# Two element-wise operations moved from POOL to VectorE, row factors in three buffers, and the feed-forward stream at two steps a turn

## The chip, the cores and the metric

The kernel runs on one core of one Trainium2 chip. The metric is the device time of one execution in microseconds (us). The kernel before took 1141.61 us, the median of 3 runs (1139.79 to 1145.35). The engines are called as in the profile: PE is TensorE (PEld its weight loads), DVE is VectorE, ACT is ScalarE, POOL is GpSimd, and SP is the engine that issues most of the loads.

## The reference

The computation is an attention with a small memory, followed by a feed-forward layer for a part of the tokens. There are 8 batches, 8 heads, 576 positions, a head size of 64 and 32 memory slots; the second part works on rows of 512 numbers, with a hidden size of 1024 and a capacity of 128 tokens for each batch.

```python
a = softmax(phi, axis=positions)            # 8 x 8 x 576 x 32
k_m = einsum('bhsm,bhsd->bhmd', a, k)       # 32 x 64 for each head
v_m = einsum('bhsm,bhsd->bhmd', a, v)
x = softmax(q @ k_m.T / 8) @ v_m            # laid out as 8 x 576 x 512
scores = x @ w_gate
for b in range(8):
    top = the 128 tokens with the highest scores[b]
    xe = x[b, top]
    out[b] = x[b]
    out[b, top] = xe + sigmoid(scores[b, top]) * (relu(xe @ w1) @ w2)
```

Which tokens are chosen depends on small differences of the scores, so the kernel computes the first softmax and `v_m` in more than plain single precision, by splitting numbers into a high and a low part.

## The kernel before, in words

The work is a set of Python generators. One main loop advances each of them by a step or a few in every turn, and the order in which they issue instructions is the program order of every engine. That order is fixed when the kernel is built: a turn is a list of work for DVE, ACT, PE, POOL and SP, and each engine walks through its own list, waiting where it needs another's result.

**The streams of a turn.**

- `softmaxes` runs the softmax over positions for 16 groups (batch and half of the heads, a tile of 128 rows by 576 positions) and then `keys`. The first 8 groups are handled by two chains with scratch of their own (`ex0`, `ex1`), taking turns; the last 8 by the first chain alone. A group takes 11 steps. Its four extended-precision multiply-adds are `fma` (L214 to L223), which use the scratch tiles `lo`, `big` and `low`: five operations on DVE, and one product on POOL (L218). DVE reads that product in L222.
- `keys` (L298) transposes the softmax on PE, copies it to `aS` on ACT, splits it on DVE into `ahi` and `alo` (L312, L314), and writes both to `aparts` in DRAM by eight transfers issued on POOL (L317). PE forms `k_m` from `aS` (L323).
- `split_v` splits `v` of a group in a high part (L285, DVE) and the rest (L287, a subtraction on POOL), and writes both to `vparts` in DRAM (L290). It takes a step every second turn while both it and the softmaxes are under way.
- `values` (run by `all_sums`) sums `v_m` for a set of two batches as a chain of small matmuls (L360), one position after the other, 8 matmuls a step. Its operands are rows of factors that SP loads in pieces of `T` = 24 positions: one transfer for `v_rows` (L340) and four for `a_rows` (L347). There are two buffers of each, and the load of the next piece is issued when a piece begins. A turn takes 7 steps of it, or 9 when the softmaxes are done. There are four sets.
- `attentions` runs a batch through `centre`, `scores`, `attend`, `rank` and `gather`, 26 steps. Two batches can be under way; the second starts 12 turns after the first, or 8 when the softmaxes are done. `attend` has an addition on POOL (L522). `gather` fetches the 128 chosen rows by an indirect transfer and appends the batch to `chosen`.
- `ffns` takes a batch from `chosen`, passes three empty steps, and runs `ffn`: transposes (L605), 16 matmuls with `w1` (L616), transposes again, 16 matmuls with `w2` (L626), an update on DVE (L629) and an indirect transfer of the rows to the output. That is about 24 steps with the empty ones. A turn takes one step of it, or two when more than one batch is waiting. What is left when the attentions are done follows without anything between.

The part of the main loop that counts here:

```python
for _ in range(STEPS + 2 * (not working)):
    next(sums, None)
...
if attend_all and next(attend_all, working) is working:
    break
for _ in range(1 + (len(chosen) > 1)):
    next(products)
```

Of the kernel before, what the change touches and what calls it, by code (L numbers as in the profile page):

```python
# [9 lines left out]
F32 = mybir.dt.float32  # L10
F16 = mybir.dt.float16
F32R = mybir.dt.float32r
# [4 lines left out]
ALU = mybir.AluOpType  # L17
# [3 lines left out]
P = 128  # L21
NC = 6
# [16 lines left out]
def kernel(  # L39
# [14 lines left out]
    nc = tc.nc  # L54
    ctx.enter_context(tc.manual_schedule())
    B, S, D = out.shape
    PT = S // NC
# [5 lines left out]
    Dh = D // H  # L63
    M = P // 4
    F = w1.shape[1]
    KD, KF = D // P, F // P
    SET = 2
    T = 24
    scale = 1.0 / Dh ** 0.5
    out_flat = out.rearrange("b s d -> (b s) d")  # L70

# [7 lines left out]
    rows = ctx.enter_context(tc.tile_pool(name="rows", bufs=1))  # L79
# [40 lines left out]

    v_rows = [rows.tile([P, T, Dh], F32R, name=f"v_rows{i}") for i in range(2)]
    a_rows = [rows.tile([P, 4, T, M], F32R, name=f"a_rows{i}") for i in range(2)]
    for t in v_rows + a_rows:
        nc.gpsimd.memset(t.bitcast(F32), 0.0)
    for t in kbd + vbd + vls:
# [50 lines left out]

    tt, stt = nc.vector.tensor_tensor, nc.vector.scalar_tensor_tensor
    soft = {}  # L180

    def softmax(i, ch):

        ex = exs[ch]

        def t(name, dtype=F32):
            return ex.tile([P, S], dtype, name=name)

        r = phis.pop(i)
        mx = ex.tile([P, 1], F32, name="mx")  # L190
# [9 lines left out]
        rh, rl = t("rh", I16), t("rl")  # L200
# [13 lines left out]
        def fma(val, h, c):  # L214


            lo, big, low = t("lo"), t("big"), t("low")
            nc.gpsimd.tensor_tensor(out=low, in0=val, in1=rl, op=ALU.mult)  # L218
            stt(out=lo, in0=val, scalar=GRID, in1=h, op0=ALU.mult, op1=ALU.subtract)  # L219
            tt(out=lo, in0=lo, in1=rh, op=ALU.mult)  # L220
            tt(out=big, in0=h, in1=rh, op=ALU.mult)
            tt(out=low, in0=low, in1=lo, op=ALU.add)  # L222
            stt(out=val, in0=big, scalar=c * UP, in1=low, op0=ALU.add, op1=ALU.add)  # L223

# [17 lines left out]
        dl, p = t("lo"), t("big")  # L242
# [35 lines left out]
    def split_v(b):  # L278

        for g in range(NG):  # L280
            vb = vio.tile([P, 4 * S * Dh // P], F32, name="vb")
            nc.sync.dma_start(out=vb, in_=v[b, g])
            yield
            hi = vio.tile([P, 4 * S * Dh // P], F32, name="vhi")
            nc.vector.tensor_single_scalar(hi.bitcast(I32), vb.bitcast(I32), -4096,  # L285
                                           op=ALU.bitwise_and)
            nc.gpsimd.tensor_sub(vb, vb, hi)  # L287
            yield
            for vp, src in enumerate((vb, hi)):
                nc.gpsimd.dma_start(  # L290
                    out=vparts[b, g, :, vp].rearrange("w r s d -> w (r s d)")
                                           .rearrange("w (p x) -> p w x", p=P),
                    in_=src.unsqueeze(1).to_broadcast([P, 2, 4 * S * Dh // P]))
            yield
# [3 lines left out]
    def keys(i, ch):  # L298
        ex, (b, g) = exs[ch], groups[i]
        a = soft.pop(i)  # L300
        kb = ks.pop(i)
        aS = ex.tile([PT, NC, P], F32, name="aS")
        for c0 in range(0, NC, 3):
            tp = bank([PT, 3, P])
            for c in range(3):
                nc.tensor.transpose(out=tp[:, c], in_=a[:, (c0 + c) * PT:(c0 + c + 1) * PT],  # L306
                                    identity=ident)
            nc.scalar.activation(aS[:, c0:c0 + 3], tp, AF.Copy)  # L308
        yield
        hi = ex.tile([PT, NC, P], F32, name="ahi")  # L310
        lo = ex.tile([PT, NC, P], F32, name="alo")
        nc.vector.tensor_single_scalar(hi.bitcast(I32), aS.bitcast(I32), -4096,  # L312
                                       op=ALU.bitwise_and)
        nc.vector.tensor_sub(lo, aS, hi)  # L314
        for part, src in enumerate((lo, hi)):
            for h in range(4):
                nc.gpsimd.dma_start(  # L317
                    out=aparts[h, b, g, part].rearrange("(c p) m -> p c m", p=PT),
                    in_=src[:, :, h * M:(h + 1) * M])
        km = bank([P, 2, 2 * M])  # L320
        for rr in range(2):
            for c in range(NC):
                nc.tensor.matmul(out=km[:, rr], lhsT=kb[:, c, rr * P:(rr + 1) * P],  # L323
                                 rhs=aS[:, c, rr * 2 * M:(rr + 1) * 2 * M],
                                 start=(c == 0), stop=(c == NC - 1))
        for u in range(2):
            part = slice(u * Dh, (u + 1) * Dh)
            nc.scalar.activation(kbd[b][part, 2 * g:2 * g + 2, u * M:(u + 1) * M],
                                 km[part, :, u * M:(u + 1) * M], AF.Copy)
# [3 lines left out]
    def values(st):  # L333

        b0 = st * SET

        def load(ch):
            nc.sync.dma_start(  # L340
                out=v_rows[ch % 2][0::2].rearrange("p s d -> p (s d)").bitcast(F32),
                in_=vparts[b0:b0 + SET].rearrange("b g t w r s d -> (b g t w r) (s d)")
                    [:, ch * T * Dh:(ch + 1) * T * Dh])
            for h in range(4):
                src = aparts[h, b0:b0 + SET].rearrange("b g t s m -> (b g t) (s m)")
                src = src[:, ch * T * M:(ch + 1) * T * M]
                nc.sync.dma_start(  # L347
                    out=a_rows[ch % 2][2 * h::8, h].rearrange("p s m -> p (s m)").bitcast(F32),
                    in_=src.unsqueeze(1).to_broadcast([4 * SET, 2, T * M]))

        n = S // T
        load(0)
        for ch in range(n):
            if ch + 1 < n:
                load(ch + 1)
            vr, ar = v_rows[ch % 2], a_rows[ch % 2]
            for s in range(T):
                for i in range(2 * SET):
                    p = slice(i * 32, i * 32 + 32)
                    nc.tensor.matmul(out=accs[i][:Dh, :P].rearrange("p (h m) -> p h m", m=M),  # L360
                                     lhsT=vr[p, s], rhs=ar[p, :, s],
                                     start=(ch == 0 and s == 0), stop=(ch == n - 1 and s == T - 1))
                if s % 2:
                    yield
        for bb in range(SET):
            v_m[b0 + bb] = const.tile([P, NPR, M], F32, name=f"v_m{b0 + bb}")
            for g in range(NG):
                for u in range(2):
                    nc.scalar.activation(
                        v_m[b0 + bb][u * Dh:(u + 1) * Dh, 2 * g:2 * g + 2],  # L370
                        accs[2 * bb + g][:Dh, :P].rearrange("p (r u m) -> p r u m", r=2, u=2)[:, :, u],
                        AF.Copy)
# [278 lines left out]
    chosen, done = [], []  # L651
# [71 lines left out]
    while True:  # L723
# [23 lines left out]
            attend_all = attentions()  # L747
        if attend_all and next(attend_all, working) is working:
            break
        for _ in range(1 + (len(chosen) > 1)):  # L750
            next(products)
    done.append(True)
    finish(products)
# [47 lines left out]
```

## Time and profile before

| | |
|---|---|
| time, median of 3 runs | 1141.61 us (1139.79 to 1145.35) |
| span of the profiled execution | 1141.4 us |
| mean granted TensorE clock | 0.805 |
| moved by the DMA engines | 156.64 MB, 137 GB/s over the span |
| SP's loads of `v_rows` / `a_rows` | 96 of 384 KB / 384 of 48 KB |
| POOL's writes of `vparts` / `aparts` | 32 of 1152 KB / 128 of 72 KB |

The profile is a record of one execution. Its page gives the busy time of each engine, the span in 40 slices with the busy share of each engine in tenths, the chain of work that ended last, and the costliest groups of instructions. A group's line reads: source line, engine, operation, tile written and tile read, shapes and count; then the busy time in us and the mean of one instruction in ns; then the idle time of the engine just before these instructions, and what ended it. The trace behind the page can be asked for a table of stages (stretches of the span, with the busy time of each engine), for waits in a stretch, and for a timeline: one line for each instruction or run of like instructions, with its start in us, its duration, and in brackets the idle time before it.

The span falls into four stages. Up to about 430 us two softmax chains run. From 430 to 845 us one chain runs beside attentions. From 845 us the softmaxes are done, and the last set of `values` runs beside the attentions of batches 4 and 5, until 1018 us. Then come the attentions of batches 6 and 7, and two feed-forward blocks, which run from 1091 to 1128 us with nothing beside them.

### The profile page before, as it was taken

The numbers are of one execution on the slowest core, as the hardware profiler recorded it, in microseconds if no ns is written. First come the engines' busy times: TensorE is split into PE (matmuls) and PEld (weight loads), VectorE is DVE, ScalarE is ACT, GpSimd is POOL, SyncE is SP. The second block draws the span as 40 slices with busy tenths as digits, with TensorE's granted clock in tenths as the row PEclk, the third lists the DMA queues.
The fourth block names the chain that finished last, engine by engine and source line by source line (L and its number), as shares of the span: only waits on it lengthen the run. The fifth ranks groups of instructions, "written<-read, shape, count | busy, mean of one in ns | idle before, by whom it ended". The sixth has DMA issues, their size and how long they took to land.

```text
span 1141.4 us, 25115 instructions
## 1 busy us (share of the span) xinstructions
PE 605.3 (53%) x10738; PEld 428.4 (38%) x10738; DVE 789.0 (69%) x1227; ACT 295.2 (26%) x577; POOL 378.9 (33%) x401
## 2 busy tenths in 40 slices
PE   0022020343425406663673747867658879779785
PEld 0022020333425304452543434636445545545442
DVE  8869779696786876979796788996961235416710
ACT  2133132121322313224132333332231112113320
POOL 7362542534535343142341331524420021203300
PEclk9999999996656655676685859876679888889888
DMA  8353543547568463343251424534334454422100
GB/s 280 114 201 141 175 146 114 172 161 263 195 233 284 177 213 82 107 152 109 82 161 37 129 92 126 157 105 118 111 75 134 123 166 149 148 74 88 56 18 22
DMA packets 52390, 156.64 MB, mean 137 GB/s; under 512 B 8880, under 2 KB 19120, under 8 KB 52272
## 3 DMA queue, kind: packets, MB, share of 16 engines
q1 hardware_dynamic: 33456, 94.13, 26.6%
q0 software_dynamic: 18816, 60.83, 15.8%
q8 instruction: 87, 1.43, 0.5%
q14 instruction: 31, 0.25, 0.1%
HBM read 96.21 MB, written 58.72 MB: 136 GB/s over the span
## 4 chain that ended last, share of the span: by engine, by line
DVE 49%; PE 21%; issue 9%; POOL 7%; DMA 5%; ACT 4%; SPq 3%; DVEq 0%; ACTq 0%; POOLq 0%
DVE lo L220 6%; PE acc L360 5%; DVE lo L219 5%; DVE low L222 4%; POOL aparts L317 4%; DMA a_rows<-aparts 3%; PE bank L616 3%; DVE num L223 3%; PE bank L626 3%; SPq L347 3%; DVE e L272 2%; DVE ph L198 2%; PE bank L323 2%; PE bank L515 2%; DVE cmp L563 2%
## 5 line engine op out<-in xcount | busy, mean ns | idle before, releaser
L360 PE MATMUL acc<-a_rows,v_rows 32*64 32x128 f32 x9216 | 221.0, 255 | 132.1 <-DMA a_rows<-aparts 129.2
L360 PEld LDWEIGHTS acc<-a_rows,v_rows 32*64 32x64 f32 x9216 | 196.3, 164 | 214.3 <-issue 120.0
L306 PE MATMUL bank<-ident,e 128*96 128x128 f32 x96 | 24.0, 421 | 281.9 <-DVE e L273 281.9
L306 PEld LDWEIGHTS bank<-ident,e 128*96 128x96 f32 x96 | 16.7, 193 | 289.1 <-issue 238.5
L218 POOL TENSOR_TENSOR low<-num,rl 128x576 f32<-128x576 f32 x48 | 74.5, 1551 | 94.3 <-DVE num L223 72.5
L522 POOL TENSOR_TENSOR xj<-xj,mean 128x1024 f32<-128x1024 f32 (+1 forms) x24 | 50.1, 2086 | 136.3 <-DVE xj L519 136.2
L287 POOL TENSOR_TENSOR vb<-vb,vhi 128x1152 f32<-128x1152 f32 x16 | 47.3, 2955 | 139.5 <-DVE vhi L285 139.4
L220 DVE TENSOR_TENSOR lo<-lo,rh 128x576 f32<-128x576 f32 x64 | 80.9, 1264 | 2.2
L222 DVE TENSOR_TENSOR low<-low,lo 128x576 f32<-128x576 f32 x64 | 48.0, 750 | 49.3 <-POOL low L218 49.3
L616 PE MATMUL bank<-w_sb,xeT 128*128 128x512 f32 x128 | 79.0, 725 | 1.4 <-ACT xeT L607 1.4
L626 PE MATMUL bank<-w_sb,hT 128*128 128x512 f32 x128 | 73.4, 686 | 0.0
L317 POOL DMA_DIRECT2D aparts<-alo x64 | 47.3, 746 | 70.6 <-DVE alo L314 49.6
L177 ACT ACTIVATE vh<-num 128x576 int16<-128x576 f32 x32 | 21.9, 683 | 180.3 <-DVE num L223 176.4
L219 DVE SCALAR_TENSOR_TENSOR lo<-num,vh 128x576 f32<-128x576 f32 x48 | 55.6, 1158 | 16.4 <-ACT vh L177 16.1
L323 PE MATMUL bank<-aS,kb 96*128 96x64 f32 x384 | 63.8, 342 | 5.5 <-ACT aS L308 5.5
L323 PEld LDWEIGHTS bank<-aS,kb 96*128 96x128 f32 x384 | 62.7, 257 | 9.0 <-ACT aS L308 7.5
L515 PE MATMUL bank<-vbd,eT 128*128 128x256 f32 x160 | 53.4, 463 | 0.0
L317 POOL DMA_DIRECT2D aparts<-ahi x64 | 46.6, 735 | 3.5 <-DMA vparts<-vhi 3.5
L563 DVE SCALAR_TENSOR_TENSOR cmp<-row,tg,wide 128x576 bf16<-128x576 f32 x40 | 39.4, 985 | 10.0 <-ACT row L549 9.2
L198 DVE SCALAR_TENSOR_TENSOR ph<-q,ph 128x576 f32<-128x576 int16 x32 | 32.1, 1003 | 13.6 <-ACT q L177 13.0
L450 DVE SCALAR_TENSOR_TENSOR eT<-es,th 128x288 f32<-128x288 f32 x32 | 17.0, 530 | 35.4 <-ACT th L448 34.5
L519 DVE TENSOR_TENSOR xj<-bank,rd 128x512 f32<-128x512 f32 x40 | 27.5, 687 | 18.5 <-PE bank L515 18.2
(146 smaller groups left out, 1231.1 us busy)
## 6 DMA issues: line engine op xcount, KB each, us to landing
v_rows<-vparts SPq DMA_DIRECT2D x96, 384.0 KB
vparts<-vb POOLq DMA_DIRECT2D x16, 1152.0 KB, 4.8
vparts<-vhi POOLq DMA_DIRECT2D x16, 1152.0 KB, 7.4
a_rows<-aparts SPq DMA_DIRECT2D x384, 48.0 KB
kb<-in_k SPq DMA_DIRECT2D x16, 576.0 KB
vb<-in_v SPq DMA_DIRECT2D x16, 576.0 KB
qb<-in_qT SPq DMA_DIRECT2D x16, 576.0 KB
out<-xj POOLq DMA_DIRECT2D x16, 512.0 KB, 4.4
```

What stands on the lines that cost most here:

```text
L198: stt(out=r, in0=q, scalar=-ln2, in1=r, op0=ALU.mult, op1=ALU.add)
L218: nc.gpsimd.tensor_tensor(out=low, in0=val, in1=rl, op=ALU.mult)
L219: stt(out=lo, in0=val, scalar=GRID, in1=h, op0=ALU.mult, op1=ALU.subtract)
L220: tt(out=lo, in0=lo, in1=rh, op=ALU.mult)
L222: tt(out=low, in0=low, in1=lo, op=ALU.add)
L317: nc.gpsimd.dma_start(out=aparts[h, b, g, part].rearrange("(c p) m -> p c m", p=PT), in_=src[:, :, h * M:(h + 1) * M])
L323: nc.tensor.matmul(out=km[:, rr], lhsT=kb[:, c, rr * P:(rr + 1) * P], rhs=aS[:, c, rr * 2 * M:(rr + 1) * 2 * M], start=(c == 0), stop=(c = ...
L360: nc.tensor.matmul(out=accs[i][:Dh, :P].rearrange("p (h m) -> p h m", m=M), lhsT=vr[p, s], rhs=ar[p, :, s], start=(ch == 0 and s == 0), st ...
L515: nc.tensor.matmul(out=o[:, g * 4 * Dh:(g + 1) * 4 * Dh], lhsT=eT[:, g, (c0 + c) * P:(c0 + c + 1) * P], rhs=vbd[b % 3][:, g], start=False, ...
L563: nc.vector.scalar_tensor_tensor(out=cmp, in0=row, scalar=g, in1=wide[:, off:off + S], op0=ALU.is_equal, op1=ALU.mult, accum_out=equal[:, ...
L616: nc.tensor.matmul(out=ps[:n], lhsT=xeT[:, d, :n], rhs=w1_sb[:, d, f0:f0 + 512], start=(d == 0), stop=(d == KD - 1))
L626: nc.tensor.matmul(out=ps[:n], lhsT=hT[:, f, :n], rhs=w2_sb[:, f], start=(f == 0), stop=(f == KF - 1))
```

## The change

The change has four parts.

1. Both element-wise operations that the softmax and the split of `v` had on POOL go to DVE: the product `low` in `fma`, which moves behind `big`, and the subtraction of `split_v`. [...]
2. The rows of factors get three buffers in place of two, with pieces of 18 positions in place of 24, and two pieces are loaded ahead. That is for PE's waits for those loads. There are 32 pieces in a set, where there were 24.
3. To make room, `aS`, `ahi` and `alo` of `keys` use the same memory as `lo`, `big` and `low` of the softmax, which become as wide as the widest use.
4. The feed-forward stream takes two steps in every turn.

```diff
-    T = 24
+    T = 18
...
-    v_rows = [rows.tile([P, T, Dh], F32R, name=f"v_rows{i}") for i in range(2)]
-    a_rows = [rows.tile([P, 4, T, M], F32R, name=f"a_rows{i}") for i in range(2)]
+    v_rows = [rows.tile([P, T, Dh], F32R, name=f"v_rows{i}") for i in range(3)]
+    a_rows = [rows.tile([P, 4, T, M], F32R, name=f"a_rows{i}") for i in range(3)]
...
+    WIDE = ("lo", "big", "low")
...
-            return ex.tile([P, S], dtype, name=name)
+
+            return ex.tile([P, NC * P if name in WIDE else S], dtype, name=name)[:, :S]
...
             lo, big, low = t("lo"), t("big"), t("low")
-            nc.gpsimd.tensor_tensor(out=low, in0=val, in1=rl, op=ALU.mult)
             stt(out=lo, in0=val, scalar=GRID, in1=h, op0=ALU.mult, op1=ALU.subtract)
             tt(out=lo, in0=lo, in1=rh, op=ALU.mult)
             tt(out=big, in0=h, in1=rh, op=ALU.mult)
+            tt(out=low, in0=val, in1=rl, op=ALU.mult)
             tt(out=low, in0=low, in1=lo, op=ALU.add)
...
-            nc.gpsimd.tensor_sub(vb, vb, hi)
+            nc.vector.tensor_sub(vb, vb, hi)
...
-        aS = ex.tile([PT, NC, P], F32, name="aS")
+        aS = ex.tile([P, NC * P], F32, name="lo")[:PT].rearrange("p (c m) -> p c m", m=P)
...
-        hi = ex.tile([PT, NC, P], F32, name="ahi")
-        lo = ex.tile([PT, NC, P], F32, name="alo")
+        hi = ex.tile([P, NC * P], F32, name="big")[:PT].rearrange("p (c m) -> p c m", m=P)
+        lo = ex.tile([P, NC * P], F32, name="low")[:PT].rearrange("p (c m) -> p c m", m=P)
...
-                out=v_rows[ch % 2][0::2].rearrange("p s d -> p (s d)").bitcast(F32),
+                out=v_rows[ch % 3][0::2].rearrange("p s d -> p (s d)").bitcast(F32),
...
-                    out=a_rows[ch % 2][2 * h::8, h].rearrange("p s m -> p (s m)").bitcast(F32),
+                    out=a_rows[ch % 3][2 * h::8, h].rearrange("p s m -> p (s m)").bitcast(F32),
...
         load(0)
+        load(1)
         for ch in range(n):
-            if ch + 1 < n:
-                load(ch + 1)
-            vr, ar = v_rows[ch % 2], a_rows[ch % 2]
+            if ch + 2 < n:
+                load(ch + 2)
+            vr, ar = v_rows[ch % 3], a_rows[ch % 3]
...
-        for _ in range(1 + (len(chosen) > 1)):
+        for _ in range(2):
             next(products)
```

## The prediction, made before the changed kernel ran

> **What bounds the kernel now.** I read the page's engine shares and its 40 slices first. DVE is the busiest engine (789.0 us of 1141.4), but in the slices its digits are 6 to 9 only up to slice 30 and fall to 1 to 6 after. So I asked for a table of four stages. Columns: stretch, length, busy us of PE, PEld, DVE, ACT, POOL, then granted clock, DMA share and GB/s.
>
> ```profile
> 0.00:430.00 430.00, 106.42 (x2544) 98.23 (x2544) 344.01 (x435) 106.61 (x175) 189.02 (x197) 0.84 0.56 190
> 430.00:845.00 415.00, 259.61 (x4678) 184.55 (x4678) 342.26 (x556) 128.65 (x255) 134.90 (x137) 0.72 0.37 109
> 845.00:1016.00 171.00, 140.29 (x3106) 93.59 (x3098) 53.83 (x122) 27.89 (x71) 29.90 (x37) 0.88 0.47 141
> 1016.00:1142.00 126.00, 98.95 (x423) 52.06 (x422) 48.87 (x115) 32.05 (x76) 25.12 (x30) 0.88 0.13 42
> ```
>
> Stages A (430 us) and B (415 us) are DVE's: busy 80% and 82%. Stage C (171 us) is PE's, busy 82%; D is a chain through DVE, POOL and PE, then PE alone.
>
> In A and B the question is what DVE's time is made of. The groups of the page:
>
> ```profile
> L218 POOL TENSOR_TENSOR low<-num,rl 128x576 f32<-128x576 f32 x48 | 74.5, 1551 | 94.3 <-DVE num L223 72.5
> ...
> L287 POOL TENSOR_TENSOR vb<-vb,vhi 128x1152 f32<-128x1152 f32 x16 | 47.3, 2955 | 139.5 <-DVE vhi L285 139.4
> L220 DVE TENSOR_TENSOR lo<-lo,rh 128x576 f32<-128x576 f32 x64 | 80.9, 1264 | 2.2
> L222 DVE TENSOR_TENSOR low<-low,lo 128x576 f32<-128x576 f32 x64 | 48.0, 750 | 49.3 <-POOL low L218 49.3
> ```
>
> L220 and L222 are the same operation on the same shape, yet L220, issued next to POOL's product, takes 1264 ns and L222 750 ns. And L222 stands idle 49.3 us for POOL. Both are seen at one place of the timelines of POOL
>
> ```profile
> 113.87 2.95 POOL L317 DMA_DIRECT2D aparts<-alo  x4 [4.50 <-DVE alo L314]
> 116.82 2.91 POOL L317 DMA_DIRECT2D aparts<-ahi  x4
> 119.74 1.41 POOL L218 TENSOR_TENSOR low<-num,rl 128x576 f32<-128x576 f32 x1
> 123.48 3.23 POOL L287 TENSOR_TENSOR vb<-vb,vhi 128x1152 f32<-128x1152 f32 x1 [2.33 <-DVE vhi L285]
> ```
>
> and of DVE:
>
> ```profile
> 121.18 0.76 DVE L222 TENSOR_TENSOR low<-low,lo 128x576 f32<-128x576 f32 x1 [5.48 <-POOL low L218]
> ...
> 124.28 3.05 DVE L220 TENSOR_TENSOR lo<-lo,rh 128x576 f32<-128x576 f32 x1
> ```
>
> The product is queued behind eight transfers that POOL issues for 5.9 us, and DVE waits 5.48 us; then L220 beside POOL's L287 takes 3.05 us in place of 0.76. All of the 49.3 us (8 waits) lie in stage A.
>
> For C, the longest of PE's waits in 845 to 1018 us (sum, times, longest):
>
> ```profile
> PE acc L360 <- DMA a_rows<-aparts: 28.3, 15, 4.0
> ```
>
> and one piece, in SP's timeline and where PE first uses it in its own:
>
> ```profile
> 933.36 0.50 SPq L340 DMA_DIRECT2D v_rows<-vparts  x1
> 933.90 2.45 SPq L347 DMA_DIRECT2D a_rows<-aparts  x4
> ```
>
> ```profile
> 940.16 1.12 PE L360 MATMUL acc<-a_rows,v_rows 32*64 32x128 f32 x32 [4.03 <-DMA a_rows<-aparts]
> ```
>
> Nearly all of PE's 31 us idle in C is for rows of factors; a load takes 5 to 7 us from the start of issue to PE's use (933.36 to 940.16). For D, PE's tail:
>
> ```profile
> 1093.43 10.01 PE L616 MATMUL bank<-w_sb,xeT 128*128 128x512 f32 x16 [0.69 <-ACT xeT L607]
> ...
> 1121.25 7.13 PE L626 MATMUL bank<-w_sb,hT 128*128 128x512 f32 x16
> ```
>
> With the lines between, these are two whole feed-forward blocks, 1091.7 to 1128.4 us, with nothing beside them.
>
> [...]
>
> **Part 1, POOL's operations to DVE.**
> Added. 64 products at 0.755 us (row L222) = 48.3 us. The trace has no 1152-wide subtraction on DVE; bounds are 1.22 us (L489, 1024 wide) and 2 x 0.755 = 1.51[...]: 16 x 1.36 = 21.8. By stage: A has 36 products and all subtractions, 27.2 + 21.8 = 49.0; B has 28 products, 21.1.
> Removed, stretching. I compare the mean of each DVE group in a stage with its undisturbed duration. A: L220 36 x (1.336 - 0.755) = 20.9; L219 27 x 0.40 = 10.8; L221 4.7; L198 18 x 0.255 = 4.6; L272 16 x 0.275 = 4.4; L314, L212, L255, L192 together 9.2; L382 1: 56 us. B: L220 28 x 0.415 = 11.6; L219 8.5 + 1.2; L221 3.5; L198 3.3; L208, L192, L563 6.9: 35 us, of which I leave 4 to POOL's L522, which stays: 31.
> Removed, waiting: 49.3 in A. DVE's other idle time in A (about 37 us: the start, ACT's conversions at 0.8 us each) I keep.
> Sum A: 49 - 56 - 49 = -56; I give back 2 for waits for ACT that the POOL wait covered: **A = 430 - 54 = 376**. B: 21 - 31 = -10.
>
> **Part 3, shared scratch, a new wait.** The next group's first `fma` writes `big` after the transfers that read `ahi` from the same memory. What is queued behind DVE's write is the whole softmax. In A the next group of the chain gets there 8 turns later (over 25 us at some 3.8 us a turn): nothing. In B it is 4 turns. From the end of L314, POOL issues for 5.9 us and the transfer lands 4.9 us later (page, DMA issues): 11 us if POOL is free. In the trace from the end of L314 to L221 it is 12 to 24 us for most groups, but in the quiet stretch after batch 1 the split ends at 672.7, POOL's issues at 679.4, landing about 684.2, and L221 starts at 683.0. So 0 to 4 us for each of 7 groups; I take 5 in sum, bounds 0 and 28. `lo` waits for PE's L323, ended 6 us or more earlier in every group I looked at: nothing.
>
> **Part 2, three buffers.** A piece is issued two pieces = 36 steps ahead in place of 24: in C that is 4 turns in place of 2.7, at 36 turns in 141 us (877 to 1018) about 15 us, less the piece just ended, against the 5 to 7 us of a load. The price is SP's: 2.95 us a piece, 32 pieces instead of 24, 94 us a set; C's last set took 138 us, so SP does not bound. Bytes are the same. Of 28 us I take 22 as gone. In B, PE's waits for rows are 35.5 us (15 waits), most of them hidden behind DVE; the chain of waits shows 4.3 us of one at 677. DVE waits for PE and ACT there in pieces of 2 to 8 us (some 60 us), and I take 7 off. In A they are hidden by DVE: nothing.
> The longer memsets at the start (three tiles of 3/4 size) cost POOL about 1 us: nothing.
>
> **Part 4, two feed-forward steps.** A block then takes 12 turns, not 24. PE's work is the same, only earlier. C has 34 + 32 of the 32-per-block matmuls, 2.06 blocks. After, half of block 2 is done in B, where PE is 63% busy, and C holds blocks 3, 4 and a third of 5: +0.25 x 16.6 us = +4, and 1 for the shorter distance (1.5 turns, not 3) from gather to use. **C = 171 - 22 + 5 = 154.** In B two steps a turn take PE some 2.2 us instead of 1.1 in nearly half of the turns; PE has 155 us idle there, but results for DVE come later; I leave the sum at nothing, bounds -3 and +15. **B = 415 - 10 + 5 - 7 = 403.**
> D: attentions 6 and 7 take 34 turns, 1018 to 1091. Batch 6 is chosen at turn 26; 8 turns x 2 steps - 3 empty = 13 of block 6's 19 steps are done when the attentions end. PE's sum before that point is as it was (before: the end of block 4 and block 5; after: most of 5, and 13 steps of 6). Left: 6 steps x 0.87 = 5.3 us and block 7 at 16.7 instead of 36.7: -15. **D = 125.4 - 15 = 110.**
>
> Sum: 376 + 403 + 154 + 110 = **1043 us**.
>
> **Rivals.**
> *Waits take the place (chance 0.22).* Without POOL's wait DVE meets ACT's conversions, A gives 35 rather than 54; the doubled feed-forward delays PE's results in B by 15 and the scratch waits are 15: A 395, B 425, C 157, D 110 = 1087. For: ACT's conversions follow each `fma` directly. Against: a second chain fills such gaps in A.
> *PE gains as well (0.17).* With fewer gaps PE's clock rises from 0.72 towards 0.88 in B, and PE's keys (L306, L323: 8% of B's chain) shorten: B 383; C at PE's busy time, 140 + 3 = 143; A 374, D 107 = 1007.
> *Slower (0.05).* Stretching is not POOL's doing and stays, and the scratch wait is the full 11 us in each of 16 groups: 1043 + 56 + 31 + 16 x 11 - 5 = 1301; with stretching gone and half the groups waiting in full, 1043 + 88 - 5 = 1126. Against: the pairs of lines above; only the extreme lies above 1141.
> My forecast has 0.56.
>
> **How the numbers follow.** 1043 is the first case. The range runs from the third case, 1007, to just under the second, 1082, and holds most of both. Faster by over 0.5% is 0.94, within 0.5% 0.02, slower 0.04.
>
> **What would show it.** Right: L220 and L219 at about 755 ns; no DVE wait for a POOL `low`; the ninth L191 near 330 us instead of 377; softmaxes done near 780; PE's waits for `a_rows` in the last set under 8 us; about 22 us from the last attention to the last L626. Wrong: DVE waiting at L221 or L222 for transfers of `aparts` over 30 us in all; SP issuing without pause in the last set; PE's L360 still waiting over 15 us in it.

## The result, and the profile after

The changed kernel takes 1062.62 us (median of 4 runs, 1059.85 to 1071.77), against 1143.48 us for the kernel before on the same chip: ratio 0.930, 95% interval 0.922 to 0.937. The prediction was 1043 us with a range of 1007 to 1082: faster, as forecast, but by 81 us and not by 98.

The stages end, here and below, at the same events in every kernel: A at the first operation on `vbig` (L390 after, L387 before), B at the last split of `keys` (L316, L314), C at the seventh `vbig`, D at the end. By these, the kernel before has 427.6, 417.2, 174.9 and 121.7 us. The table of stages of the changed kernel (columns as before):

```profile
0.00:374.40 374.40, 107.74 (x2544) 99.02 (x2544) 336.22 (x481) 106.86 (x175) 88.57 (x147) 0.84 0.65 219
374.40:790.90 416.50, 267.93 (x4700) 197.10 (x4702) 341.31 (x591) 130.49 (x258) 86.63 (x109) 0.70 0.38 109
790.90:948.10 157.20, 138.55 (x3202) 97.67 (x3198) 55.27 (x123) 28.63 (x75) 31.07 (x38) 0.87 0.52 152
948.10:1060.20 112.10, 88.62 (x302) 47.04 (x302) 48.65 (x114) 29.00 (x70) 25.88 (x30) 0.83 0.14 47
```

| stage | forecast | measured |
|---|---|---|
| A | -54 | -53.2 |
| B | -12 | -0.7 |
| C | -17 | -17.7 |
| D | -15 | -9.6 |
| sum | -98 | -81.2 |

So almost all that is missing is missing in B. The groups of the page that answer to those of before (L221 is the old L220, L224 the old L222):

```profile
L221 DVE TENSOR_TENSOR lo<-lo,rh 128x576 f32<-128x576 f32 x64 | 52.4, 819 | 2.2
L224 DVE TENSOR_TENSOR low<-low,lo 128x576 f32<-128x576 f32 x64 | 48.5, 758 | 2.2
```

The idle time before L224 is 2.2 us where it was 49.3, and L221's mean is 819 ns where it was 1264. It isn't 758 everywhere, and the same group taken stage by stage says where. The first three lines are of A, the last is of B:

```profile
L221 DVE TENSOR_TENSOR lo<-lo,rh 128x576 f32<-128x576 f32 x36 | 27.3, 758 | 1.2
L223 DVE TENSOR_TENSOR low<-num,rl 128x576 f32<-128x576 f32 x27 | 20.3, 751 | 0.0
L289 DVE TENSOR_TENSOR vb<-vb,vhi 128x1152 f32<-128x1152 f32 x16 | 21.7, 1358 | 0.6
...
L221 DVE TENSOR_TENSOR lo<-lo,rh 128x576 f32<-128x576 f32 x28 | 25.1, 898 | 1.0
```

In A the stretching is gone; in B some is left. The two moved operations have the sizes that were taken for them: 751 ns for the product and 1358 ns for the subtraction. The author's estimate for it, 1.36 us, lies midway between the prediction's two bounds from the trace, 1.22 and 1.51 us. DVE's timeline in A now runs through without a gap at the places where it waited for POOL:

```profile
111.67 1.36 DVE L289 TENSOR_TENSOR vb<-vb,vhi 128x1152 f32<-128x1152 f32 x1
112.94 0.75 DVE L220 SCALAR_TENSOR_TENSOR lo<-num,vh 128x576 f32<-128x576 f32 x1
113.73 0.76 DVE L221 TENSOR_TENSOR lo<-lo,rh 128x576 f32<-128x576 f32 x1
114.40 0.75 DVE L222 TENSOR_TENSOR big<-vh,rh 128x576 f32<-128x576 int16 x1
115.07 0.75 DVE L223 TENSOR_TENSOR low<-num,rl 128x576 f32<-128x576 f32 x1
115.86 0.76 DVE L224 TENSOR_TENSOR low<-low,lo 128x576 f32<-128x576 f32 x1
```

PE's waits in C (sum, times, longest): those for rows fell from 28.3 to 12.7 us, and one for the rows that `gather` fetched is new.

```profile
PE acc L363 <- DMA a_rows<-aparts: 12.7, 12, 2.2
PE bank L608 <- DMA xe<-out,idx: 4.8, 2, 3.7
```

In the middle of the last set, from 865 to 909 us, SP issues one piece after the other with hardly a pause. Over all of C it still waits 33.1 us for PE to free a buffer. That wait, and one piece:

```profile
SPq L342 <- PE acc L363: 33.1, 13, 14.9
```

```profile
875.20 0.50 SPq L342 DMA_DIRECT2D v_rows<-vparts  x1
875.75 2.45 SPq L349 DMA_DIRECT2D a_rows<-aparts  x4
```

PE's tail, behind the last list of chosen rows at 1028.31, is 23.5 us (before: 1089.92 to 1128.31, 38.4 us):

```profile
1028.21 7.13 PE L629 MATMUL bank<-w_sb,hT 128*128 128x512 f32 x16
...
1036.46 7.13 PE L619 MATMUL bank<-w_sb,xeT 128*128 128x512 f32 x16 [0.69 <-ACT xeT L610]
...
1044.78 7.13 PE L629 MATMUL bank<-w_sb,hT 128*128 128x512 f32 x16
```

### The profile page after: what moved, and what is told of

It is laid out like the page before. It is cut to its first block, busy times and chain, and to the rows that moved or that the text cites. A ratio compares the mean times of both kernels' runs of the same rounds, so it can differ in the third digit from the quotient of the medians.

```text
span 1060.2 us, 25334 instructions
## 1 busy us (share of the span) xinstructions
PE 602.8 (57%) x10738; PEld 440.8 (42%) x10738; DVE 781.4 (74%) x1307; ACT 295.0 (28%) x577; POOL 232.2 (22%) x323
## 4 chain that ended last, share of the span: by engine, by line
DVE 53%; PE 22%; DMA 7%; issue 6%; ACT 5%; SPq 3%; POOL 2%; DVEq 0%; ACTq 0%; POOLq 0%
PE acc L363 5%; DVE low L224 4%; PE bank L629 4%; DVE lo L220 4%; DVE big L222 4%; DVE low L223 4%; DVE lo L221 3%; PE bank L619 3%; DVE num L225 3%; SPq L349 3%; PE bank L325 2%; DMA a_rows<-aparts 2%; DVE e L274 2%; DVE ph L200 2%; PE bank L518 2%
## 5 line engine op out<-in xcount | busy, mean ns | idle before, releaser
L319 POOL DMA_DIRECT2D aparts<-low x64 | 47.7, 752 | 144.0 <-DVE low L316 121.9
L325 PE MATMUL bank<-lo,kb 96*128 96x64 f32 x384 | 68.9, 361 | 6.9 <-ACT lo L310 6.9
L325 PEld LDWEIGHTS bank<-lo,kb 96*128 96x128 f32 x384 | 67.3, 274 | 10.4 <-ACT lo L310 8.9
L619 PE MATMUL bank<-w_sb,xeT 128*128 128x512 f32 x128 | 66.3, 650 | 3.3 <-ACT xeT L610 3.3
L518 PE MATMUL bank<-vbd,eT 128*128 128x256 f32 x160 | 59.7, 508 | 0.0
L221 DVE TENSOR_TENSOR lo<-lo,rh 128x576 f32<-128x576 f32 x64 | 52.4, 819 | 2.2
L292 POOL DMA_DIRECT2D vparts<-vb x16 | 11.7, 731 | 187.9 <-DVE vb L289 162.8
L224 DVE TENSOR_TENSOR low<-low,lo 128x576 f32<-128x576 f32 x64 | 48.5, 758 | 2.2
L220 DVE SCALAR_TENSOR_TENSOR lo<-num,vh 128x576 f32<-128x576 f32 x48 | 37.2, 775 | 16.2 <-ACT vh L177 16.1
L319 POOL DMA_DIRECT2D aparts<-big x64 | 46.9, 740 | 0.0
L518 PEld LDWEIGHTS bank<-vbd,eT 128*128 128x128 f32 x160 | 34.6, 240 | 16.9 <-issue 12.9
L492 DVE TENSOR_TENSOR prod<-xj,wg 128x1024 f32<-128x1024 f32 (+1 forms) x24 | 25.0, 1041 | 21.1 <-POOL xj L525 21.1
L200 DVE SCALAR_TENSOR_TENSOR ph<-q,ph 128x576 f32<-128x576 int16 x32 | 27.4, 855 | 16.8 <-ACT q L177 16.2
L522 DVE TENSOR_TENSOR xj<-bank,rd 128x512 f32<-128x512 f32 x40 | 27.5, 686 | 14.6 <-PE bank L518 13.9
```

The lines of the kernel that those rows point to most:

```text
L200: stt(out=r, in0=q, scalar=-ln2, in1=r, op0=ALU.mult, op1=ALU.add)
L319: nc.gpsimd.dma_start(out=aparts[h, b, g, part].rearrange("(c p) m -> p c m", p=PT), in_=src[:, :, h * M:(h + 1) * M])
L518: nc.tensor.matmul(out=o[:, g * 4 * Dh:(g + 1) * 4 * Dh], lhsT=eT[:, g, (c0 + c) * P:(c0 + c + 1) * P], rhs=vbd[b % 3][:, g], start=False, ...
L619: nc.tensor.matmul(out=ps[:n], lhsT=xeT[:, d, :n], rhs=w1_sb[:, d, f0:f0 + 512], start=(d == 0), stop=(d == KD - 1))
```

## The experiments

The times are medians; ratios are to the kernel before, on the same chip. Stages come from one profile each. Profiles of kernels whose code up to the end of B is the same differ by up to 8 us in B (405.8 and 398.1 in two versions below), so small differences there are read from DVE's busy time, which repeats within 2.5 us (342.5 and 340.1 in the two that differ most). C lies between 149.7 and 159.4 us in the seven profiles with the changed kernel's row buffers and two feed-forward steps in it. In A, three versions (`x_dve`, `half_d`, `ffn_end`) have a start that is 3.4 us shorter, though their code there is that of the changed kernel; the last section shows it.

**Part 1 undone, whole and by half.** First both operations are put back on POOL, then the product alone.

```diff
-            tt(out=low, in0=val, in1=rl, op=ALU.mult)
+            nc.gpsimd.tensor_tensor(out=low, in0=val, in1=rl, op=ALU.mult)   # ahead of lo, as before
...
-            nc.vector.tensor_sub(vb, vb, hi)
+            nc.gpsimd.tensor_sub(vb, vb, hi)                                 # first version only
```

> The changed kernel with both operations back on POOL (product and subtraction of v). My theory: A +54 as forecast; in B the product on DVE costs 21 us and saves about 22 of stretching, so B changes by under 4 us: span 1112 to 1118. Rival (my forecast's sizes: B wins 10 by the move, and something else took it back): B +10, span about 1124.

> The changed kernel with the product alone back on POOL; the subtraction of v stays on DVE. Stage A is 374 us with both on DVE and 431 with both on POOL. My theory (the product carries nearly all of it: its queue 49, its stretching about 36 x 0.84 = 30, its cost on DVE 27; the subtraction saves 24 of stretching for 22 of DVE's time): A 425 to 430, B as in the kernel before, span about 1113. Rival (the subtraction, 2.96 us each on POOL, holds up the product behind it and stretches DVE most): A 395 to 410, span 1085 to 1098.

Measured: both back, 1119.31 us, 0.980 (0.975 to 0.984), A 431.2, B 418.8. Product alone back, 1098.59 us, 0.964 (0.960 to 0.968), A 409.8, B 419.2, which is the rival's case. DVE's wait in A with the product alone on POOL:

```profile
DVE low L224 <- POOL low L220: 43.2, 8, 7.6
```

So in A the subtraction is worth 21 us (431.2 to 409.8) and the product 35 (409.8 to 374.4), by different ways. Moving the subtraction leaves that wait at 43 us (it was 53.0 with both on POOL). DVE's busy time falls from 343.0 to 331.6 although 21.7 us of subtractions are added, so 33 us of stretching go with it. Moving the product adds 27 us, DVE is busy 336.2 instead of 331.6, and the wait goes. In B both moves together bring 2 us: DVE's busy time goes from 343.9 to 341.3 with 21.1 us added, so 24 us of stretching went there, and not the 31 forecast.

**The queue alone.** In the kernel before, ACT issues the transfers of `aparts`, so that POOL's product isn't queued behind them. Nothing else is changed.

```diff
-                nc.gpsimd.dma_start(
+                nc.scalar.dma_start(
                     out=aparts[h ...
```

> The kernel before, with one edit: the eight transfers of keys to aparts (L317) are issued by ACT and not by POOL. Product and subtraction stay on POOL, so DVE is stretched as before, but the product is no longer queued behind 5.9 us of issuing. My theory (in stage A the waiting and the stretching are two separate costs of about 49 and 55 us, and the first comes from that queue): DVE's wait for low falls from 49 to under 8 us, A 428 -> 385 with 5 us given back since ACT now issues in front of the softmax's conversions; span about 1098. Rival (the product is late because POOL itself is slow, or ACT's issuing delays DVE as much as POOL's did): A stays above 415, span over 1128.

Measured: 1132.47 us, 0.994 (0.992 to 0.996); A 415.1, as the rival had it. DVE's waits in A:

```profile
DVE lo L219 <- ACT vh L177: 33.0, 16, 6.9
DVE vhi L285 <- DMA vb<-in_v: 13.3, 2, 10.8
...
DVE low L222 <- POOL low L218: 2.2, 1, 2.2
```

The wait for POOL falls from 49.3 to 2.2 us, so it was the transfers ahead of the product, not the product, that DVE waited for. But A gives only 12.5 us: the queue now stands before ACT's conversions (33.0 us where it was 11.7), DVE's wait for `vb` doubles (13.3 us where it was 6.2), and its busy time rises from 341.8 to 347.9. In B the transfers hold up ACT's conversions as well: DVE's wait at L198 is 29.2 us where it was 12.3, and B is 426.1 us instead of 417.2. C is 8.7 us shorter in this profile (166.2 instead of 174.9), for a reason that wasn't looked for. A wait moved from one engine's queue to another's is not a wait removed.

**POOL's last operation beside DVE in B.** The changed kernel with the addition of the mean in `attend` on DVE too.

```diff
-            nc.gpsimd.tensor_add(x, x, row.unsqueeze(1).to_broadcast([P, cols, D]))
+            nc.vector.tensor_add(x, x, row.unsqueeze(1).to_broadcast([P, cols, D]))
```

> The changed kernel with the last element-wise tensor operation of POOL, the addition of the mean in attend (L525, 24 times), on DVE too. My theory (what stretching is left in B is this addition's: L221 898 ns, L200 982, L210 1019, L194 887, L391 1230 there, some 17 us in all): these go to their durations of stage A (about 755, 574, 170), DVE takes 8 x 1.22 + 4 x 0.69 = 12.5 us more in B and stops waiting 9 us for the sum: B -13; D -4, since 1.22 us replaces 2.4 us in a chain of six: span about 1043. Rival (the stretching in B comes from POOL issuing transfers): the means stay, B +3, span about 1060.

Measured: 1041.93 us (1039.4 to 1046.89), 0.912 (0.908 to 0.917), the best version of this study and faster than the changed kernel. B is 405.8 instead of 416.5; two later versions with this edit have 402.0 and 398.1, while B lies between 411.0 and 419.2 in the nine profiles of changed kernels with the addition on POOL. A, where the edit changes nothing, is 4.6 us shorter, 3.4 of it by the start. The groups of DVE in B, after:

```profile
L221 DVE TENSOR_TENSOR lo<-lo,rh 128x576 f32<-128x576 f32 x28 | 25.1, 898 | 1.0
...
L200 DVE SCALAR_TENSOR_TENSOR ph<-q,ph 128x576 f32<-128x576 int16 x14 | 13.7, 982 | 15.7 <-ACT q L177 15.5
...
L492 DVE TENSOR_TENSOR prod<-xj,wg 128x1024 f32<-128x1024 f32 x8 | 9.7, 1217 | 9.0 <-POOL xj L525 9.0
```

and with this edit:

```profile
L221 DVE TENSOR_TENSOR lo<-lo,rh 128x576 f32<-128x576 f32 x28 | 21.2, 758 | 1.0
...
L200 DVE SCALAR_TENSOR_TENSOR ph<-q,ph 128x576 f32<-128x576 int16 x14 | 10.5, 749 | 12.3 <-ACT q L177 12.1
L525 DVE TENSOR_TENSOR xj<-xj,mean 128x1024 f32<-128x1024 f32 x8 | 9.8, 1225 | 0.3
L492 DVE TENSOR_TENSOR prod<-xj,wg 128x1024 f32<-128x1024 f32 x8 | 9.7, 1217 | 0.0
```

12.6 us of additions come to DVE, and yet it is busy 3.6 us less (337.7 instead of 341.3): some 16 us of stretching in B were this one operation's, where the prediction had left it 4. The 9.0 us that DVE stood waiting for it are gone too.

**ACT's order in B.** DVE waits 10.2 us in B for `gr` from ACT (L592), behind two copies into `kbd` that `keys` gives to ACT. Here those copies are issued a turn later.

```diff
-        for u in range(2):
-            ...
-            nc.scalar.activation(kbd[b][part, ...], km[part, ...], AF.Copy)
+        copies_due.append((turn_now[0] + 1, copies))
...
             next(products)
+        while copies_due and copies_due[0][0] <= turn:
+            copies_due.pop(0)[1]()
```

> The changed kernel with ACT's copies of k_m to kbd issued one turn later, at the turn's end. In stage B, ACT stands 37 us (7 times, up to 11.1) at these copies for PE's matmuls L325, and behind them are the conversions that DVE waits for (15.5 us at L200, 10.2 at L597). My theory (this queue on ACT is a main part of the 75 us that DVE is idle in B, which no part of the change touched): those two waits fall under 8 us in sum, B 417 -> 400, the rest unchanged, span about 1044. Rival (B is set by PE, which is late at the same places; ACT's order does not matter): B within 5 us, span 1056 to 1062.

Measured: 1060.73 us, 0.932 (0.927 to 0.937); B 415.9. DVE's waits there (lines are four higher in this kernel):

```profile
DVE prod L496 <- POOL xj L529: 13.3, 3, 6.5
...
DVE gr L601 <- ACT gr L596: 2.3, 3, 1.9
```

The wait for `gr` falls by 8 us and the one for POOL's addition rises by 4; the stage doesn't move beyond its spread, as the rival had it. This wait was not what set B's length.

**The rows.** The changed kernel with two buffers, pieces of 24 and one piece ahead, as before; then with four buffers, pieces of 12 and three ahead, which is 48 pieces a set.

```diff
-    T = 18
+    T = 24                      # second version: T = 12
...
-        load(1)
...
-            if ch + 2 < n:
-                load(ch + 2)
+            if ch + 1 < n:
+                load(ch + 1)    # second version: three ahead, four buffers
```

> The changed kernel with two buffers of rows, pieces of 24 and one piece ahead, as before; the shared scratch stays. My theory (the buffers pay in stage C only): PE's waits for a_rows in the last set rise from 13 to about 28 us, C 156 -> 172, A and B unchanged: span about 1076. Rival 1 (they pay in B as well, as I forecast): B +7 more, 1083. Rival 2 (SP's 32 rather than 24 pieces a set had replaced PE's waits by SP's issue time, so nothing was won): C within 4 us, span 1060.

> The changed kernel with rows in four buffers of 12 positions, three pieces ahead: the same 36 steps ahead, the same memory, but 48 pieces a set instead of 32. My theory (with two thirds of C's last set spent issuing, SP is near its limit: 32 pieces x 2.95 = 94 of 122 us; 48 pieces x 2.95 = 142 us would set the time): the set takes 142 to 150 us, C 157 -> 178 to 190, and SP issues without a pause. A and B, where a turn is 4 to 5 us and takes 7 steps, have room (3.45 us of issuing for 12 steps... 1.7 us a turn): unchanged. Span about 1085. Rival (SP has room, since pieces and transfers get smaller and issue faster): C within 6 us, span about 1063.

Measured: two buffers, 1082.67 us, 0.945 (0.938 to 0.952), C 181.1 instead of 157.2, B 417.4. Four buffers, 1128.97 us, 0.988 (0.984 to 0.992), A 402.0, C 198.7. PE's waits in C, with two buffers (lines one lower):

```profile
PE acc L362 <- DMA a_rows<-aparts: 28.4, 13, 4.6
```

So the third buffer is worth 24 us of C and nothing that can be read in B. The medians say the same: they differ by 20 us, no more than C alone. With pieces of 12, PE waits in 23 pieces, 33.0 us in all, although each load is asked for just as many positions ahead: there are more of them. A piece takes SP 2.95 us here too, so 48 pieces are 142 us for a set, and other loads pass through the same queue. Here SP is at its limit: it waits for PE 6.4 us in C, where it was 33.1, and issuing on SP is 14% of the page's chain, where it was 3%. That also explains A, which I had expected to stay. DVE's waits there:

```profile
DVE vhi L287 <- DMA vb<-in_v: 19.4, 3, 10.7
...
DVE vhi L287 <- DMA aparts<-big: 8.3, 1, 8.3
```

The first was 6.5 us in the changed kernel. SP loads `vb` as well, behind the row loads in its order. Its timeline shows it for the longest of these waits: SP issues rows up to 375.2 us, issues `vb` at 375.26, and L287 begins at 379.71, after 10.70 us of waiting.

**The feed-forward stream.** The rule of before in the changed kernel; then two steps only once the last `v_m` is summed, which is D alone.

```diff
-        for _ in range(2):
+        for _ in range(1 + (len(chosen) > 1)):
+        # second version: range(2 if len(summed) == B else 1 + (len(chosen) > 1))
             next(products)
```

> The changed kernel with the feed-forward stream as before: one step a turn, two only when more than one batch waits. The stages of the changed kernel are A 374, B 417, C 156, D 113 us (span 1060). My theory (the doubled step pays in the tail and costs little elsewhere): D +15 with two whole blocks at the end again, C -4 (half a block less in it, part of another more), B within 4 us: span about 1070. Rival (two steps a turn put PE late in stage B and ate the gain that I forecast there): B falls by 10 to 15 us, so the span stays at 1055 to 1062 although D grows.

> The changed kernel with two feed-forward steps a turn only once all sums over positions are done (stage D), and one step before. With one step throughout, C was 148 and D 120 us; with two, C 157 and D 112. My theory (two steps cost C 9 us, by more of PE's work in it and by waits for rows that were just gathered, 4.8 us, and win D 8 us): C 148, D 113, span 1051. Rival (D's gain comes only from the work that C had done ahead): C 148, D 120, span 1058.

Measured: rule of before, 1061.05 us, 0.929 (0.924 to 0.934), stages 374.6, 415.5, 148.3, 119.9. Neither expectation met these stages: C gives 9 us and not 4, D costs 8 and not 15, and B stays. Two steps in D alone, 1051.89 us, 0.923 (0.919 to 0.927), stages 371.9, 411.5, 146.6, 118.8. So the fourth part as a whole brings nothing that can be measured: it gives 7.8 us in D and takes 8.9 in C. Of the second version's 11 us, C gives 10.6 and D takes 6.7. A is 2.5 us shorter, though its code is that of the changed kernel, and its start is 3.4 us shorter. B, whose code is that of the version with the rule of before, is 5.0 us shorter than in the changed kernel and 4.0 shorter than there, within its spread. The intervals of the two ratios overlap, so a gain isn't established. Its D is as long as with the rule of before, as the rival had it, because more is then left over for D: 66 records of feed-forward matmuls lie between the seventh `vbig` and the last list of chosen rows, against 48 with the rule of before and 49 in the changed kernel. (Such counts are of records in the trace. One fp32 matmul of the code shows as two of them: `ffn` issues 8 matmuls with `w1`, and the timeline of PE's tail above lists 16 for a block at L619. The numbers of matmuls given for a block ahead of the result are such records too.)

In C the two-step stream costs what PE has more to do (138.5 us busy instead of 134) and the wait for the gathered rows that is shown above, 4.8 us, which the rule of before doesn't have. In D the stretch from the seventh `vbig` to the last list of chosen rows is 80.2 us instead of 69.7, though it holds as many records of feed-forward matmuls (49 against 48). One of PE's groups in it, with the rule of before:

```profile
L518 PE MATMUL bank<-vbd,eT 128*128 128x256 f32 x40 | 12.3, 432 | 0.0
```

and with two steps:

```profile
L518 PE MATMUL bank<-vbd,eT 128*128 128x256 f32 x40 | 15.1, 513 | 0.0
```

The same instructions take PE longer: it is busy 65.8 us instead of 57.6 at a granted clock of 0.79 instead of 0.93. The slow ones of L518 lie together, where the burst of block 5 is over and block 6 has not begun. PE's timeline there, after:

```profile
998.77 2.08 PE L518 MATMUL bank<-vbd,eT 128*128 128x256 f32 x4
```

But these are not where the time is lost. The chain of waits through the stretch can be compared piece by piece. Some of its lines, with two steps:

```profile
949.72 2.61 PE bank L619 x4
...
952.76 2.58 PE bank L619 x4
...
971.68 0.79 PE bank L507 x8
...
1006.63 2.37 PE bank L585 x10
...
1009.69 4.64 DMA xe<-out,idx
```

and with the rule of before:

```profile
953.46 0.79 PE bank L507 x8
...
988.21 2.08 PE bank L585 x10
```

From the seventh `vbig` to L507, the first matmuls of `attend`, it is 23.5 us with two steps (948.15 to 971.68) and 15.1 with the rule of before (938.39 to 953.46). Feed-forward matmuls take 16.3 and 7.9 us of the chain there, 32 records against 16: that is the whole difference of 8.4 us. From L507 to L585 of block 6, where the slow L518 lie, it is 35.0 and 34.8 us. From there to the last list it is 21.7 and 19.8 us; the chain now goes through the fetching of block 6's rows (4.64 us). So the burst standing ahead of the attention makes the stretch longer. The lower clock has a small part in it: the first eight records of the burst take 5.2 us, where a later four take 1.72 (granted clock 0.70 from 949.7 to 955.3 us, 1.00 from 955.7 to 968), so some 1.8 us by this estimate.

**Keeping PE's clock up.** Can the lower clock in D be avoided, and is it worth it? In three versions, each empty step of the feed-forward stream in D issues an extra matmul whose result nothing reads: 512 columns in the changed kernel; 512 together with `x_dve` and `ffn_end`; 256 together with `x_dve`.

```diff
+    def warm():
+        if len(summed) == B:
+            ps = bank([P, 512], pool=pss)      # third version: 256, also in rhs
+            nc.tensor.matmul(out=ps, lhsT=ident, rhs=w1_sb[:, 0, :512], start=True, stop=True)
...
             else:
+                warm()
                 yield
...
                 for _ in range(3):
+                    warm()
                     yield
```

> The changed kernel with one extra 128x512 matmul, whose result nobody reads, in each empty step of the feed-forward stream in stage D; nothing else. With two steps a turn the stretch from the seventh centring to the last choice takes 80.2 us, with one step 69.7, although PE has the same work up to there; in it, the trace has L518 at 2.08 us for four matmuls against 1.13, once PE has no feed-forward work between. My theory (bunching the feed-forward leaves PE with so little in between that its clock falls, and the attention's matmuls, which are on the chain, take twice as long): the extra work keeps L518 at 1.13, the stretch falls to 70 to 73 us and D from 112 to 103 to 106: span about 1053. Rival (pairs of feed-forward steps stand in front of the attention's matmuls in PE's order): the extra 18 to 36 matmuls at 0.44 us only add, the stretch is 80 to 92, D 112 to 122.

> All that the runs point to: the changed kernel with the addition of the mean on DVE too, one feed-forward step a turn before stage D and two in it, and the extra matmuls in D's empty steps. My theory: A 370, B 404, C 146, D 100 to 106 us, span 1020 to 1026. Rival (the parts take from each other, as the addition's 5 us in D lay in the same chain that the clock slowed): D 110, span 1030 to 1036.

> The changed kernel with the mean's addition in attend (L525) on DVE, and with one extra, unread matmul of 128x256 (half the width of the earlier trial) in each empty step of the feed-forward stream while the last two batches are attended; its result is used nowhere, the outputs are as before. To be held against the version without these extra matmuls: 1041.93 us, 0.9123 of the kernel before, last stage 107.8 us, of which 75.8 from the seventh vbig to the last list of chosen rows, TensorE's clock in that stage 0.86. Theory, an idle TensorE costs the last stage time because its clock drops: the 128x512 trial restored the clock, but its 20 us of extra matmuls stood in the way; at half the dose the clock is at least 0.93, the four matmuls of L518 take 1.13 us and not 2.08, the stretch to the last list is 68 to 72 us, the last stage 100 to 104, the whole 1034 to 1038 (ratio 0.905 to 0.909). Rival, the clock is only seen to drop where TensorE waits for DVE and ACT anyway, and what it would save is less than what the extra matmuls take: the stretch is 76 to 82 us, the last stage 108 to 114, the whole 1042 to 1049 (ratio 0.912 to 0.919).

Measured: 1073.16 us, 0.940 (0.937 to 0.944), D 121.0 against 112.1 without; 1053.31 us, 0.923 (0.920 to 0.925), D 124.1 (118.8 in `ffn_end`, which has the addition on POOL); 1046.98 us, 0.918 (0.916 to 0.921), D 112.3 against 107.8. PE's groups between the seventh `vbig` and the last list of chosen rows, with the 256 columns:

```profile
L659 PE MATMUL bank<-w_sb,ident 128*128 128x256 f32 x65 | 19.2, 429 | 0.0
...
L518 PE MATMUL bank<-vbd,eT 128*128 128x256 f32 x40 | 12.3, 432 | 0.0
```

The clock is 0.94 there instead of 0.84, and L518 is back at 432 ns, where it was 490 without. PE's busy time without the extra matmuls is 74.1 - 19.2 = 54.9 us, where it was 64.7. So PE's clock is lower in this stretch where it has no extra matmuls to do, and its work there takes about 10 us longer. But the stretch is 79.2 us instead of 75.7: the extra matmuls took 19.2 us (31.7 us at 512 columns: each is two records in the trace, which I had counted as one), and these stand ahead of the attention's own on PE's queue. That the extra matmuls raise the clock in this stretch is shown; that the time of D could be won back in this way is not. In the first and the third run the rival's figures held; in the second, D's 124.1 us and the time lie beyond the rival's as well. The chain agrees: the burst up to L507 is 1.4 us shorter with the extra matmuls (22.1 us instead of 23.5), and what follows is 4.9 us longer.

## Why the prediction was right, and where not

**A, right.** The three terms held: 48.7 us added where 49.0 was forecast (the operations took 751 and 1358 ns), stretching removed of 54 us (DVE's busy time went from 341.8 to 336.2 with 48.7 added; 56 was forecast), and the wait for POOL gone (49.3 us before, none in DVE's waits after). The ninth softmax's first operation is at 328.5 us, forecast "near 330". The first rival's "DVE meets ACT's conversions" did not come: that wait is 11.7 us before and after.

**B, the step that failed.** Of -10 + 5 - 7 = -12 only -0.7 came. The mechanism of the first term was right and its size wrong: "35 us, of which I leave 4 to POOL's L522, which stays". It was 16 us (the run with that addition on DVE), so the move took 24 and not 31 off, and gained 2 to 3 where -10 was forecast. The prediction had split the stretching by which POOL operation each DVE line is issued next to; POOL's addition takes 2.4 us and lies beside whatever DVE does in that time, L221 and L200 as well. The "-7" for the rows was taken from the chain of waits and from PE's 35 us of waiting, and the two-buffer run gives less than 1 us in B, where B's spread is several us: PE waited, but B's end did not wait for PE. The "+5" of the shared scratch is one wait of 1.5 us:

```profile
DVE big L222 <- DMA aparts<-big: 1.5, 1, 1.5
```

The case of the "slower" rival, 11 us in each of 16 groups, is far from it. The first rival had B at 425, near the measured 416.5, but for a reason that did not happen: without the doubled feed-forward B is 415.5.

**C, right in sum, with luck.** Rows: 24 us against 22. Doubled feed-forward: 8.9 against 5. The reasoning for the rows took positions for steps. A step is two positions, so "36 steps ahead" are 18 steps: 2 of C's turns and not 4, some 8 us at 3.9 us a turn and not "about 15", against the 5 to 7 us of a load. The margin was small, which fits the waits that are left. Its "+4" of more blocks in C is right (4.4 us more of PE's busy time); the "1 for the shorter distance from gather to use" is a wait of 4.8 us. The signs given in advance were mixed: PE's waits for `a_rows` are 12.7 us where "under 8" was to show success, and SP issues nearly without pause in the middle of the set, which was named as a sign of failure. But over C it still waits 33.1 us for PE. SP isn't at its limit with pieces of 18; it is with pieces of 12.

**D, right in its tail only.** "-15" was the tail, and the tail is shorter by 14.9 us. The step "PE's sum before that point is as it was" failed. The number of records is as it was (241 against 240), but they lie elsewhere: the burst of block 5 stands ahead of the attention's matmuls, on the chain, and where PE then waits for DVE it has no feed-forward work to fill in. PE is busy 65.8 us instead of 58.5, at a clock of 0.79 instead of 0.92, and the stretch before that point is 10.0 us longer (70.2 to 80.2). Another 4.7 us came by luck at the very end, from PE's last matmul to the end of the span (13.1 to 8.4), for which the prediction had no term: 10.0 - 14.9 - 4.7 = -9.6. That end is 12.4 to 15.0 us in all kernels with the feed-forward rule of before in C, and 8.3 to 8.8 in the others. At the kernel's last line SP waits 4.1 to 6.0 us for PE's sequencer in the former and 0.9 us in the latter; what holds PE's sequencer isn't shown.

**The rivals.** "PE gains as well" needed a clock in B towards 0.88; it is 0.70, down from 0.72. That fewer gaps raise the clock was supposed there, and the stages of before do not show it: A has 0.84 with PE busy for a quarter of it, B 0.72 with 63%. The result, 1062.6, lies between the forecast and the first rival, and by neither's mechanism alone: it is the forecast with B's gain left out and D's cut. One reading was off without a consequence: DVE's digits after slice 30 are 0 to 7 and not 1 to 6.

## What to carry to other kernels

When an engine is stretched by a neighbour, take all of the neighbour's operations off that stage or count what each of them overlaps in time; the last one left can keep half of the stretching (16 of 35 us here), and moving that one shortened the stage by 11 us more although it gave the busiest engine more work. An engine's wait may be for what is queued ahead of its producer, here eight transfers (without them DVE's wait went from 49.3 to 2.2 us); moving those to another queue moved the wait, because that queue was waited for as well (33.0 us instead of 11.7). Work that is done earlier is not free because its sum is the same: look at what it displaces in the stage where it now lies, and at the gap that it leaves behind (here 241 records of PE took 80.2 us to the last list where 240 had taken 70.2).

## What was not expected of the hardware

- A stretched DVE operation ends a fixed time after POOL's operation, however early it began. In the kernel before, 62 of DVE's operations on 128x576 elements with two tensor inputs, among those that the timeline lists singly, begin while one of POOL's element-wise operations runs. All 62 end 0.60 to 0.63 us after it. Two more begin together with POOL's operation or 0.02 us before it; they keep their 0.76 and 0.75 us. The place that the prediction shows goes on on POOL and on DVE, where L221 ends at 129.20, 0.62 us after POOL's product:

```profile
126.67 1.91 POOL L218 TENSOR_TENSOR low<-num,rl 128x576 f32<-128x576 f32 x1
```

```profile
127.25 1.95 DVE L221 TENSOR_TENSOR big<-vh,rh 128x576 f32<-128x576 int16 x1
```

  So the price is what is left of POOL's operation when DVE's turn comes; by what way POOL holds DVE isn't shown. In all, POOL's 16 subtractions, 47.0 us busy, cost DVE 33 us in A; the products in A, 54.6 us busy, cost it 22; the additions in B, 25.2 us busy, cost it some 16.
- At the start, POOL clears the buffers for some 13 us (1.26 to 14.41 us in the changed kernel). DVE's first two instructions, of 2 us or less, then last until that is over in most kernels, and in three they do not. DVE's timeline of the changed kernel,

```profile
1.35 13.14 DVE L145 CAST ident<-ident 128x128 bf16<-128x128 f32 x1 [1.35 <-POOL ident masks.py:199]
3.72 10.77 DVE L193 TENSOR_REDUCE mx<-ph 128x1 f32<-128x576 f32 x1
```

  and of the version with the addition on DVE, whose code here is the same:

```profile
1.35 2.04 DVE L145 CAST ident<-ident 128x128 bf16<-128x128 f32 x1 [1.35 <-POOL ident masks.py:199]
3.76 0.75 DVE L193 TENSOR_REDUCE mx<-ph 128x1 f32<-128x576 f32 x1 [0.36 <-DMA ph<-in_phiT]
```

  The second softmax starts at 44.2 us instead of 47.5. In the kernel before, L145 took 12.11 us: the longer memsets of the second part, which the prediction costed at nothing, are 1 us on DVE's path. Why the two cases differ was not found.
- Four records of L518 on PE take 2.08 us in a sparse stretch and 1.13 us in a dense one (granted clock 0.51 from 988 to 1012 us with PE busy 66%, 1.00 from 972.5 to 985 with 96%). An extra fp32 matmul of 128x256 shows as two records of 429 ns (clock 0.94), one of 128x512 as two of 601 ns (clock 1.00): half the width took 29% off a record.
- SP issues the four transfers of `a_rows` in 2.45 us and the one of `v_rows` in 0.50 us, in pieces of 24, 18 and 12 positions alike. Here that limits how small a piece may be, as 48 pieces are 142 us of issuing for a set: pieces of 18 in three buffers took 24 us off C, held against pieces of 24 in two, and pieces of 12 in four added 41.
